# Issuing SyncE's first load before its register moves and before ScalarE's small load

## The chip, the cores and the metric

The kernel runs on one core of one Trainium2 chip. The metric is device time in microseconds (us) of that core. The profiled spans are some 2 us shorter than the timed executions (130.3 against 132.57 us in before). A span here runs from the first instruction of the trace to the last.

## The reference, cut to what matters

The program is an attention block over a set of points (through 32 "inducing" rows) and a feed-forward block with GELU. Only the shapes matter for the change: `x` is 4 x 12480 x 128 in float32, 25.6 MB, it is read once, and an output of the same size is written.

```python
I = np.broadcast_to(inducing[None], (B, m, C))       # m = 32 rows of C = 128
h = mab(I, x)                                        # the inducing rows attend to x
y = mab(x, h)                                        # x attends to the result
# ... then on all 49920 rows: gelu(y @ w_in) @ w_out, w_in 128 x 2048
```

## The kernel before

The first transfers are the subject. The first "pair" of `x` is 32 blocks of 128 rows. SyncE loads half of it in float32 as `x_first`, VectorE casts this half to float16, and GpSimd's queue loads the other half, casting on the way. GpSimd then loads a second pair, and ScalarE loads the small `inducing`.

```python
src = units[0][0].rows_of(x_rows)
nc.sync.dma_start(out=x_first[:, :16, :], in_=src[:, :16, :])      # L295, 1 MB
nc.gpsimd.dma_start(out=x_pair[:, 16:, :], in_=src[:, 16:, :])     # L296, cast on the way
a_load(units[0][2])                                                # L287, GpSimd
# ... identity ...
nc.scalar.dma_start(out=ind_s, in_=inducing)                       # L305, 16 KB
nc.tensor.transpose(indT_ps, ind_s, identity[:M, :M])              # L307
# ... constants on VectorE, 8 warm-up matmuls on TensorE (fill, L359),
#     two casts of x_first (a_cast, L363), then transposes of x (L377) ...
```

The instructions are generated first and reordered afterwards, by a function of the kernel's own source: `loads_ahead` takes the first load or loads of an engine out of the body and puts them into the program's entry block, ahead of the barrier with which the program opens. For each engine it says how many loads, and in front of the first instruction of which kind:

```python
for engine, n, kind in (
    (ET.SP, 1, mybir.InstDrain),
    (ET.Activation, 1, mybir.InstDrain),
    (ET.Pool, 2, mybir.InstEventSemaphore),
):
    moves = [i for i in rest if i.engine == engine][:n]
    ...
    at = min(k for k, i in enumerate(head)
             if i.engine == engine and isinstance(i, kind))   # layout shortened
    head[at:at] = moves
```

In the raw records of before SyncE runs four register moves (at 0.000, 0.070, 0.136 and 0.186 us), then the load (0.256), then the drain that belongs to the barrier (0.691). The results were correct with the load on either side of the moves.

Of the kernel before, what the change touches and what calls it, by code (L numbers as in the profile page):

```python
# [248 lines left out]
def kernel(  # L249
# [742 lines left out]
    with tc.If(flag > 0, preferred_fallthrough_block=False):  # L992
        general(tc, x, moe_w_in, moe_w_out, out, ind_s, identity)
    nc.at_finalize(loads_ahead)
    nc.at_finalize(last_waits_last)
    ET = mybir.EngineType
# [10 lines left out]
def loads_ahead(nc):  # L1007



    entry, body = nc.main_func.blocks[:2]
    head, rest = list(entry.instructions), list(body.instructions)
    ET = mybir.EngineType
    for engine, n, kind in (
        (ET.SP, 1, mybir.InstDrain),
        (ET.Activation, 1, mybir.InstDrain),
        (ET.Pool, 2, mybir.InstEventSemaphore),
    ):
        moves = [i for i in rest if i.engine == engine][:n]
        for i in moves:  # L1020
            assert isinstance(i, mybir.InstDMACopy)
            rest.remove(i)
        at = min(
            k
            for k, i in enumerate(head)
            if i.engine == engine and isinstance(i, kind)
        )
        head[at:at] = moves
    entry.instructions, body.instructions = head, rest
# [296 lines left out]
```

## Time and profile before

| | before |
|---|---|
| time, median of 5 runs | 132.57 us (132.43 to 132.61) |
| profiled span | 130.3 us |
| SyncE's load: issued / first packet / mean landing | 0.256 / 1.257 / 5.24 us |
| GpSimd's first load: first packet / mean landing | 4.795 / 7.79 us |
| last store landed | 130.07 us |

The profile lines that the prediction rests on are shown with it, below. "Issue" of a load is the length of its instruction on the engine that issues it (0.377 us for SyncE's load in before); its data move as packets, which the page counts on 16 transfer engines (128 packets of 8192 bytes for this load). In the raw records such a load has 16 completion records of 4 bytes and 9 ns, and 16 landings, and "mean landing" above is the mean of these 16 times. The GB/s column counts bytes written: GpSimd's load, which casts to float16, shows about half the rate of SyncE's plain one at the same use of the engines (4096 bytes in 0.324 us against 8192 in 0.309). And in a table of stretches a packet counts, with its whole length and all its bytes, in the stretch in which it starts; in a short stretch where packets are slow, the share and the rate are then too high.

### The profile page before, as it was taken

What the parts mean: (1) busy time and instruction counts of PE and PEld (TensorE: products, weight loads), DVE (VectorE), ACT (ScalarE), POOL (GpSimd) and SP (SyncE); (2) the same over time, 40 slices, a digit from 0 to 9 for tenths busy, and PEclk for the clock granted to TensorE, in tenths of its full rate; (3) what the DMA queues carried; (4) which work ended last, traced back from release to release, by engine and by line L of the source; (5) the groups of instructions that cost most, each with busy time, mean ns of one, the idle gap of its engine ahead of it and who ended that gap; (6) DMA issues with size and microseconds to landing.
All of it is one profiled execution on the core that took longest, in us unless ns stands there. A gap on an engine that the chain in (4) does not pass through costs nothing. (4 is left out here: it accounts for less than half of the span.)

```text
span 130.3 us, 3507 instructions
## 1 busy us (share of the span) xinstructions
PE 99.2 (76%) x1365; PEld 57.5 (44%) x1365; DVE 91.6 (70%) x265; ACT 77.1 (59%) x177; POOL 65.2 (50%) x85
## 2 busy tenths in 40 slices
PE   0954878549999999999789899999996698860000
PEld 0342656349465547656544664655453413310000
DVE  1836257432699997999999977999999757993000
ACT  3007064416756888578968889798996285960000
POOL 7910113019453836895753679765198842770000
PEclk9999599965799999999999999999999657998555
DMA  4999999999999999999999999999999999999993
GB/s 131 311 228 214 211 206 211 229 209 214 224 199 219 221 211 322 322 380 377 302 324 330 310 220 288 340 367 418 443 424 419 407 453 418 405 428 430 428 418 125
DMA packets 5666, 40.17 MB, mean 308 GB/s; under 512 B 624, under 2 KB 1936, under 8 KB 2192
## 3 DMA queue, kind: packets, MB, share of 16 engines
q0 software_dynamic: 2848, 13.30, 50.1%
q1 hardware_dynamic: 2752, 26.61, 48.9%
q8 instruction: 11, 0.18, 0.5%
q10 hardware_dynamic: 48, 0.02, 0.1%
q14 instruction: 7, 0.06, 0.1%
HBM read 27.67 MB, written 25.56 MB: 409 GB/s over the span
## 5 line engine op out<-in xcount | busy, mean ns | idle before, releaser
L702 POOL TENSOR_TENSOR pair<-pair,rr 128x512 f32<-128x512 f32 x26 | 26.8, 1042 | 20.6 <-ACT pair L365 17.7
L686 PE MATMUL at<-q,e 128*128 128x512 f16 (+1 forms) x104 | 33.4, 389 | 3.8 <-DVE xT L363 1.2
L377 PE MATMUL tr<-identity_h,xh 128*128 128x128 f16 x392 | 30.3, 232 | 3.3 <-DMA xh<-in_x_dram 3.3
L377 PEld LDWEIGHTS <-xh 128*128 128x128 f16 x392 | 25.2, 105 | 9.9 <-DMA xh<-in_x_dram 4.8
L363 DVE COPY xT<-tr 128x1024 f16<-128x1024 f16 (+1 forms) x36 | 22.6, 645 | 8.9 <-PE tr L377 8.3
L365 ACT ACTIVATE xT<-tr 128x1024 f16<-128x1024 f16 (+1 forms) x16 | 15.7, 980 | 16.5 <-PE tr L377 16.5
L717 DVE TENSOR_TENSOR pair<-at,rr 128x512 f32<-128x512 f32 x36 | 23.3, 676 | 1.1 <-PE at L686 0.4
L287 POOL DMA_DIRECT2D xh<-in_x_dram x15 | 8.3, 555 | 21.4 <-DMA xh<-in_x_dram 14.2
L403 ACT ACTIVATE e<-s 128x512 f16<-128x512 f32 (+1 forms) x28 | 15.3, 546 | 5.6 <-PE s L391 5.1
L638 ACT ACTIVATE e<-s 128x512 f16<-128x512 f32 (+1 forms) x28 | 15.0, 563 | 3.6 <-PE s L626 1.8
L365 ACT ACTIVATE pair<-at 128x512 f32<-128x512 f32 x26 | 15.6, 600 | 1.6 <-PE at L686 1.0
L686 PEld LDWEIGHTS <-e 128*128 128x128 f16 (+1 forms) x104 | 8.7, 103 | 10.3 <-issue 6.9
L417 DVE STREAM_TRANSPOSE e1t<-e 128x256 int32<-128x256 int32 (+1 forms) x28 | 11.1, 399 | 3.0 <-ACT e L403 2.9
L572 POOL TENSOR_TENSOR pt<-pt 128x512 f32<-128x512 f32 (+4 forms) x20 | 12.0, 602 | 2.1 <-DVE rr L661 0.7
L425 PE MATMUL hun<-xh,e1t 128*32 128x128 f16 x392 | 10.7, 225 | 3.1 <-DVE e1t L417 3.0
L717 DVE TENSOR_TENSOR o<-at,rr 128x512 f32<-128x512 f32 (+1 forms) x19 | 10.5, 580 | 3.0 <-PE at L686 2.6
L391 PE MATMUL s<-xT,indT 128*32 128x512 f16 (+1 forms) x108 | 10.5, 376 | 1.6 <-ACT xT L365 0.8
L626 PE MATMUL s<-xT,hT 128*32 128x512 f16 (+1 forms) x100 | 10.2, 417 | 0.5 <-DVE rr L661 0.5
L425 PEld LDWEIGHTS <-e1t 128*32 128x32 f16 x392 | 6.3, 97 | 8.9 <-DVE e1t L417 6.5
L702 POOL TENSOR_TENSOR o<-o,rr 128x512 f32<-128x512 f32 x7 | 7.3, 1042 | 5.4 <-ACT o L365 3.0
L650 PEld LDWEIGHTS <-e 128*128 128x128 f16 (+1 forms) x104 | 5.6, 99 | 4.4 <-issue 1.7
L650 PE MATMUL r<-strand,e 128*128 128x4 f16 (+1 forms) x104 | 6.8, 168 | 0.0
(76 smaller groups left out, 100.6 us busy)
## 6 DMA issues: line engine op xcount, KB each, us to landing
out_dram<-pair SPq DMA_DIRECT2D x8, 2048.0 KB, 15.1
xh<-in_x_dram POOLq DMA_DIRECT2D x11, 1024.0 KB, 28.1
out_dram<-o SPq DMA_DIRECT2D x6, 1024.0 KB, 10.7
out_dram<-spent SPq DMA_DIRECT2D x1, 2048.0 KB, 18.3
x_first<-in_x_dram SPq DMA_DIRECT2D x1, 1024.0 KB, 5.2
xh<-in_x_dram POOLq DMA_DIRECT2D x1, 512.0 KB, 7.1
w_in_h<-in_moe_w_in_dram POOLq DMA_DIRECT2D x1, 512.0 KB, 17.4
w_out_h<-in_moe_w_out_dram POOLq DMA_DIRECT2D x1, 512.0 KB, 19.4
```

Of the source, the lines that this page charges most:

```text
L363: nc.vector.tensor_copy(out=out, in_=in_)
L365: nc.scalar.activation(out=out, in_=in_, func=AF.Copy)
L377: nc.tensor.transpose(tr[:, c - c0, : u.p], xh[: u.p, c, :], identity_h[: u.p, : u.p])
L403: nc.scalar.activation(out=e1[: u.p, : u.nc // 2, :, :], in_=s1[: u.p, : u.nc, :].rearrange("r (a b) i -> r a i b", b=2), func=AF.Exp, sca ...
L417: nc.vector.transpose(out=pairs(e1t)[: u.p, :n], in_=pairs(e1)[: u.p, :n])
L425: nc.tensor.matmul(bt.hun[32 * j : 32 * j + 32, :], e1t[: u.p, c // 2, :, c % 2], xh[: u.p, c, :], start=u.idx == 0 and c < 4, stop=c + 4 ...
L572: nc.gpsimd.tensor_tensor(out=bt.pt[:, :, :, :half], in0=bt.pt[:, :, :, :half], in1=bt.pt[:, :, :, half : 2 * half], op=ALU.add,)
L638: nc.scalar.activation(out=e2[: u.rows, : u.cols], in_=s2[: u.rows, : u.cols], func=AF.Exp, scale=SCALE,)
L650: nc.tensor.matmul(r2[: u.p, ci, : u.nj], e2[: u.rows, ci * u.p : (ci + 1) * u.p], strand[: u.rows, : u.nj], start=True, stop=True,)
L686: nc.tensor.matmul(at[: u.p, : u.nj, :], e2[: u.rows, ci * u.p : (ci + 1) * u.p], bt.q[: u.rows, : u.nj, :], start=True, stop=True,)
L702: nc.gpsimd.tensor_tensor(out=part, in0=part, in1=rr2[: u.p, ci, : u.nj].unsqueeze(2).broadcast_to([u.p, u.nj, 128]), op=ALU.mult,)
L717: nc.vector.tensor_tensor(out=ov[: u.p, ci, :, :], in0=at[: u.p, : u.nj, :], in1=rr2[: u.p, ci, : u.nj].unsqueeze(2).broadcast_to([u.p, u. ...
```

## The change

Its intent is that the program's longest stream, its transfers, starts with its own first load as early as possible: SyncE's load no longer stands behind four register moves, and ScalarE's small load, which used to be issued first, comes second.

```diff
     for engine, n, kind in (
-        (ET.SP, 1, mybir.InstDrain),
+        (ET.SP, 1, mybir.InstRegisterMove),
         (ET.Activation, 1, mybir.InstDrain),
         (ET.Pool, 2, mybir.InstEventSemaphore),
     ):
```

## The prediction

The 0.62 us from the end of an issue to the first packet is the trace's own, the gain comes to 0.256 - 0.06 = 0.20 us, and the weighted time to 132.4 us. Rival (a) supposes that GpSimd's first load can't begin before about 4.8 us, whatever goes before it.

> **What bounds the kernel now.** I read the page first: the engine line, then the DMA rows of the forty slices, then the table of stretches, then the opening and the end in the timeline.
>
> ```profile
> PE 99.2 (76%) x1365; PEld 57.5 (44%) x1365; DVE 91.6 (70%) x265; ACT 77.1 (59%) x177; POOL 65.2 (50%) x85
> ...
> DMA  4999999999999999999999999999999999999993
> ...
> HBM read 27.67 MB, written 25.56 MB: 409 GB/s over the span
> ```
>
> No compute engine is over 76% busy, while the DMA row is full in every slice but the first and the last. The table of stretches gives the share of each (columns: stretch and its length, five engines, granted clock, DMA share, GB/s):
>
> ```profile
> 0.00:1.00 1.00, 0.00 (x0) 0.00 (x0) 0.00 (x0) 0.00 (x0) 0.20 (x4) 1.00 0.00 0
> 1.00:2.00 1.00, 0.00 (x0) 0.00 (x0) 0.18 (x1) 0.00 (x0) 0.93 (x2) 1.00 0.50 92
> 2.00:3.00 1.00, 0.00 (x0) 0.00 (x1) 0.16 (x2) 0.87 (x1) 0.93 (x4) 1.00 0.84 260
> 3.00:5.00 2.00, 1.97 (x6) 0.83 (x7) 1.38 (x14) 0.41 (x1) 2.00 (x4) 1.00 0.97 381
> 5.00:10.00 5.00, 3.56 (x37) 2.15 (x35) 2.88 (x14) 0.21 (x1) 1.91 (x4) 1.00 1.08 223
> ...
> 88.00:126.00 38.00, 24.98 (x237) 10.97 (x234) 26.62 (x82) 21.32 (x55) 18.49 (x20) 0.82 1.01 426
> 126.00:131.00 5.00, 0.00 (x0) 0.00 (x0) 0.00 (x0) 0.00 (x0) 0.00 (x0) 0.50 0.40 162
> ```
>
> The 16 transfer engines idle for the first 1.2 us, ramp to about 2.5 us, and are then full until 126 us (shares over 1.00 are packets that overlap on an engine). The end is theirs too:
>
> ```profile
> 118.70 0.14 DVE failed L979
> ...
> SPq L1321 <- DMA out_dram<-o: 4.2, 2, 2.4
> ```
>
> The first line is the last piece of the chain of compute, over at 118.84 us; the second, from SyncE's own waits, shows it waiting for output stores to land. In the raw records the last store is issued at 118.0 and its last landing is at 130.07, with the span over at 130.28. So the compute chain is some 10 us ahead of the stores, and the program lasts as long as one unbroken stream of transfers: when that stream starts, plus its work. Only the opening can be changed by this edit.
>
> **The opening.** From the timeline (start, length, engine, line, operation):
>
> ```profile
> 0.14 0.42 ACTq L305 DMA_DIRECT2D ind_s<-in_inducing_dram  x1
> ...
> 0.26 0.38 SPq L295 DMA_DIRECT2D x_first<-in_x_dram  x1
> ...
> 1.07 0.72 POOL L296 DMA_DIRECT2D xh<-in_x_dram  x1 [0.61 <-issue]
> ...
> 5.50 1.37 DVE L363 CAST xh<-x_first 128x1024 f16<-128x1024 f32 x2
> ...
> 8.23 1.79 PEld L377 LDWEIGHTS <-xh 128*128 128x128 f16 x32 [2.30 <-DMA xh<-in_x_dram]
> ```
>
> The reader is to see that the changed load is issued at 0.26 and lands just before 5.5, but that the first transposes start only at 8.23, when GpSimd's first load has landed as well. The list of issues says the same:
>
> ```profile
> x_first<-in_x_dram SPq DMA_DIRECT2D x1, 1024.0 KB, 5.2
> xh<-in_x_dram POOLq DMA_DIRECT2D x1, 512.0 KB, 7.1
> ...
> ind_s<-in_inducing_dram ACTq DMA_DIRECT2D x1, 16.0 KB, 2.8
> ```
>
> [...] if one counts from the end of the issue: SyncE's ends at 0.633 and its first packet starts at 1.257, 0.62 us later; ScalarE's ends at 0.562, first packet at 1.187, again 0.62. [...] x_first gives each engine eight 8 KB pieces of 309 ns, they run back to back, and GpSimd's queue starts on an engine only after x_first's completion record there (15 of the 16 engines: 6 ns after). [...] Here SyncE's issue begins inside ScalarE's and takes 0.377 us against some 0.33 us for later lone stores[...].
>
> **The change part by part.** The instruction streams of the five engines are the same in kind and number. On SyncE alone the load steps over four register moves. In the raw records these start at 0.000, 0.070, 0.136 and 0.186 us and take 40, 42, 29 and 29 ns; with the gaps between them the load starts at 0.256.
>
> - Removed ahead of the load: 0.256 us. It should start at about 0.00, its issue end at 0.38, its first packet start at 0.38 + 0.62 = 1.00 instead of 1.257.
> - Added after it: the same four moves, some 0.2 us, before SyncE's drain for the opening barrier. The drain starts at 0.691 now and would start at about the same time. The barrier is collected by GpSimd at 1.496, so nothing there moves.
> - Moved: the small load of ScalarE, issued at 0.137, becomes the second one. It has 32 pieces of 512 bytes, two for each engine, at about 25 ns. Before, they ran in the ramp, where engines were idle anyway. Now they may run behind x_first. Cost in the full stream: 2 x 25 ns + a completion record of 9 ns = 0.06 us on each engine.
>
> If the whole stream slides with its first load, the gain is 0.256 - 0.06 = 0.20 us, or 0.15% of 132.57. It goes through to the end undiminished, because from 2.5 to 126 us there is no idle stretch to swallow it.
>
> Off the path: x_first landing 0.26 us earlier lets VectorE cast earlier, but the transposes wait for GpSimd's load. What shifts those is that load's turn on the engines.
>
> **The rivals.** (a) *GpSimd's first load is not ready.* [...] x_first ending at 4.6 merely leaves the engines idle. Against: its issue ends at 1.79, long before, and 15 engines took it up within 6 ns. For: one engine wrote x_first's completion record at 4.389, and no packet of GpSimd's queue starts anywhere before 4.795, so that engine stood idle for at least 0.4 us with work that should have been there. This would leave 132.5 to 132.6.
>
> (b) *The ramp shortens as well.* The 128 packets of x_first took 45.6 us of engine time against 128 x 0.309 = 39.6 at full rate, and from 1.187 to 2.5 us the engines were only 50% busy: seven began near 1.2, nine not before 2.1, and on those nine a piece of ind_s comes first. If ind_s holds them up, having x_first ahead could win up to half of the 0.65 us lost there: 132.0 to 132.2. Against: pieces of ind_s taking 0.2 to 1.0 us instead of 25 ns look like slow first accesses, which whoever comes first must pay.
>
> (c) *ind_s comes late.* Behind x_first's eight pieces it could land near 5.2 instead of 2.9 us. TensorE transposes it before its eight warm-up matmuls (3.55 us), which end at 6.8 now and have 1.4 us to spare before 8.23; VectorE's set-up and two casts follow the same transposition and end at 6.87. A delay of 2.2 us would push the first transposes back by 0.8 us. But the median x load lands 28 us after its issue, so its queue has many transfers waiting, and the stores are 10 us behind compute: the stream would not run dry. Cost at the end near zero, at worst 0.3 us (132.6 to 132.8).
>
> (d) A share of more than 2% would be 2.65 us, more than the whole of the opening up to full rate. Nothing here has that size.
>
> **Range and chances.** I give half to the clean slide (132.35 to 132.4), 0.3 to rival (a) at about 132.55, 0.1 to (b) at 132.1 and 0.1 to (c) at 132.7: the weighted time is 0.5 x 132.37 + 0.3 x 132.55 + 0.1 x 132.1 + 0.1 x 132.7 = 132.4. Three runs of before spread over 0.18 us, so the range must have that on both sides: 132.1 to 132.7. Within 2% is all but sure: 0.99, with 0.005 for each side.
>
> **What would show it right or wrong.** Right: x_first issued at 0.0, its first packet near 1.0, landed near 5.2; GpSimd's first packets near 4.55; its landing and the first transposes near 8.0; the last store landing 0.2 us earlier; DMA rows otherwise the same. Rival (a): GpSimd's first packets still at 4.8, with an idle gap before. Rival (b): all engines at work before 2 us. Rival (c): ind_s landing after 4.5 us and the first transposes no earlier than 8.3. The prediction is wrong if the end moves by more than 0.4 us either way, or if the load's first packet does not move with its issue.

## The result, and the profile after

The changed kernel took 132.77 us (median of 5, 132.34 to 132.95) against 132.57. The outputs are right. The ratio is 1.0014, with a 95% interval of 0.9994 to 1.0033. A ratio in this document is the mean time of one kernel's fast runs over the mean of the other's in the same rounds, so it is not quite the ratio of the medians quoted. This is "within 2%", as predicted, but 0.07 us outside the predicted range and with no sign of the gain of 0.2 us.

The page of the kernel after, engines, transfer row and bytes:

```profile
PE 98.7 (75%) x1365; PEld 58.6 (45%) x1365; DVE 91.5 (70%) x265; ACT 76.9 (59%) x177; POOL 65.6 (50%) x85
...
DMA  6999999999999999999999999999999999999992
...
HBM read 27.67 MB, written 25.56 MB: 407 GB/s over the span
```

The first digit of the transfer row went from 4 to 6: the engines do start earlier. The last went from 3 to 2, and nothing else moved. The table of stretches of the kernel after (same columns as in the prediction):

```profile
1.00:2.00 1.00, 0.00 (x0) 0.00 (x0) 0.19 (x1) 0.00 (x0) 0.94 (x2) 1.00 0.98 221
2.00:3.00 1.00, 0.00 (x0) 0.00 (x0) 0.16 (x2) 0.88 (x1) 0.92 (x4) 1.00 0.93 331
...
5.00:10.00 5.00, 4.95 (x35) 2.40 (x36) 3.64 (x26) 0.00 (x0) 1.79 (x4) 1.00 1.04 204
...
126.00:131.00 5.00, 0.00 (x0) 0.00 (x0) 0.00 (x0) 0.00 (x0) 0.00 (x0) 0.50 0.43 177
```

By this table the engines were 98% busy instead of 50% from 1 to 2 us, and moved 221 GB/s instead of 92. Shared out over the time in which each packet ran, it is 76% instead of 31%, and 168 GB/s instead of 66. So the first microseconds were won. But from 5 to 10 us, with the same loads and a share that reads full in both, the rate was 204 GB/s instead of 223 (197 instead of 216, shared out). The timeline of the kernel after:

```profile
0.00 0.38 SPq L295 DMA_DIRECT2D x_first<-in_x_dram  x1
0.12 0.39 ACTq L305 DMA_DIRECT2D ind_s<-in_inducing_dram  x1
...
1.06 0.72 POOL L296 DMA_DIRECT2D xh<-in_x_dram  x1 [0.61 <-issue]
...
4.70 0.28 PE L307 MATMUL indT_ps<-identity,ind_s 32*128 32x32 f32 x1 [4.70 <-DMA ind_s<-in_inducing_dram]
...
6.99 0.68 DVE L363 CAST xh<-x_first 128x1024 f16<-128x1024 f32 x1
...
8.52 1.79 PEld L377 LDWEIGHTS <-xh 128*128 128x128 f16 x32 [0.93 <-DMA xh<-in_x_dram]
```

The load is issued at 0.00, but the first transposes of `x` start at 8.52, which is 0.29 us later than in this trace of before (a second one, before2, has 8.99), and they still wait for GpSimd's load. The list of issues (columns: tile, queue, KB, median us from issue to landing) shows which loads became slower:

```profile
x_first<-in_x_dram SPq DMA_DIRECT2D x1, 1024.0 KB, 5.2
xh<-in_x_dram POOLq DMA_DIRECT2D x1, 512.0 KB, 7.4
...
ind_s<-in_inducing_dram ACTq DMA_DIRECT2D x1, 16.0 KB, 4.4
```

GpSimd's first load takes 7.4 us instead of 7.1 and the small one 4.4 instead of 2.8. The end is as it was: the chain of compute of the kernel after is over at 119.6 us,

```profile
119.48 0.14 DVE failed L979
```

and SyncE's waits again end with output stores, some 10 us later:

```profile
SPq L1321 <- DMA out_dram<-o: 4.2, 2, 2.4
```

**From the raw packet records.** The following is my own working on the records of single packets.

*Packets.* In both kernels GpSimd's first load is 128 packets of 4096 written bytes, and a packet usually takes 0.324 us. Before, the median was 0.324 and the longest 0.516. After, the median was 0.326, but eleven took over 0.6 and the longest 1.394. I call time above 0.324 per packet the *excess*: 0.8 engine-us before, 8.8 after. One engine-us is one of the 16 engines for 1 us, so the excess of 8 more is 0.5 us of the whole stream.

*Account of the opening.* From 1 to 9 us I add up what the 16 engines lost, by idling and by packets slower than their usual time:

| kernel | issue of x_first (us) | idle | slow packets | lost in all (engine-us) |
|---|---|---|---|---|
| before | 0.256 | 14.2 | 6.4 | 20.6 |
| after | 0.000 | 4.6 | 18.8 | 23.4 |

Idling fell by 9.6 engine-us (0.60 us for each engine), and slow packets rose by 12.4 (0.77 us). So the earlier start was used up within the first 9 us. A plainer count, of all time above the median of a packet's queue and size, gives nearly the same: 14.4 idle and 7.0 slow before, 4.9 and 19.8 after.

*Work curve.* I give each packet the usual time of its queue and size, add these up over the program, and compare the times at which two kernels have done the same work. After led before by 0.22 us at 5.6 us. At 8.7 us it was 0.09 behind, and from 12 to 45 us it was a constant 0.14 behind.

### The profile page after: what moved, and what is told of

Its sections match the earlier page's. It is cut to its first block, busy times and chain, and to the rows that moved or that the text cites. A ratio compares the mean times of both kernels' runs of the same rounds, so it can differ in the third digit from the quotient of the medians.

```text
span 130.9 us, 3507 instructions
## 1 busy us (share of the span) xinstructions
PE 98.7 (75%) x1365; PEld 58.6 (45%) x1365; DVE 91.5 (70%) x265; ACT 76.9 (59%) x177; POOL 65.6 (50%) x85
## 5 line engine op out<-in xcount | busy, mean ns | idle before, releaser
L702 POOL TENSOR_TENSOR pair<-pair,rr 128x512 f32<-128x512 f32 x26 | 26.8, 1042 | 19.6 <-ACT pair L365 16.7
L686 PE MATMUL at<-q,e 128*128 128x512 f16 (+1 forms) x104 | 32.4, 378 | 3.5 <-DVE xT L363 1.2
L377 PE MATMUL tr<-identity_h,xh 128*128 128x128 f16 x392 | 31.2, 236 | 3.2 <-DMA xh<-in_x_dram 3.1
L377 PEld LDWEIGHTS <-xh 128*128 128x128 f16 x392 | 26.0, 106 | 9.8 <-DMA xh<-in_x_dram 4.8
L365 ACT ACTIVATE xT<-tr 128x1024 f16<-128x1024 f16 (+1 forms) x16 | 15.7, 980 | 18.2 <-PE tr L377 18.1
L425 PE MATMUL hun<-xh,e1t 128*32 128x128 f16 x392 | 11.2, 233 | 3.0 <-DVE e1t L417 3.0
L626 PE MATMUL s<-xT,hT 128*32 128x512 f16 (+1 forms) x100 | 9.3, 380 | 0.5 <-DVE rr L661 0.5
## 6 DMA issues: line engine op xcount, KB each, us to landing
out_dram<-o SPq DMA_DIRECT2D x6, 1024.0 KB, 10.2
w_out_h<-in_moe_w_out_dram POOLq DMA_DIRECT2D x1, 512.0 KB, 19.2
```

Source lines behind the costliest of these rows:

```text
L365: nc.scalar.activation(out=out, in_=in_, func=AF.Copy)
L377: nc.tensor.transpose(tr[:, c - c0, : u.p], xh[: u.p, c, :], identity_h[: u.p, : u.p])
L425: nc.tensor.matmul(bt.hun[32 * j : 32 * j + 32, :], e1t[: u.p, c // 2, :, c % 2], xh[: u.p, c, :], start=u.idx == 0 and c < 4, stop=c + 4 ...
L686: nc.tensor.matmul(at[: u.p, : u.nj, :], e2[: u.rows, ci * u.p : (ci + 1) * u.p], bt.q[: u.rows, : u.nj, :], start=True, stop=True,)
L702: nc.gpsimd.tensor_tensor(out=part, in0=part, in1=rr2[: u.p, ci, : u.nj].unsqueeze(2).broadcast_to([u.p, u.nj, 128]), op=ALU.mult,)
```

## The experiments

**Theories.** T1: the slide was there, and scatter hid it. T2, rival (a) of the prediction: GpSimd's queue isn't ready until about 4.8 us. T3: the small load, now moved in among the pieces of `x_first`, or the later set-up work that follows from it, costs what the slide gains. T4: packets early in a stream are slow, and a stream that starts earlier has more of them; the start moves, but not the moment at which the full rate is reached. All four are suppositions for the runs to test.

The texts before each run use other names. "Readiness" is T2, "set-up" is T3, and "cold access" is a stricter T4: a fixed stock of slow first packets, paid by whoever comes first. From sp_mid on they add a fifth, "early take-up", here T5: GpSimd's packets are slow when its load is taken up too soon after its issue. It is T2 in a weaker form: the queue can be used early, but not at full speed.

The eighteen runs went in five sets, each on one chip together with runs of the kernel before, whose medians were 132.53, 132.57, 132.50, 132.52 and 132.46 us. Idle and slow engine-us are those of the account above, always from 1 to 9 us.

### The same two kernels again: before2, after2, after3

No edit. This tells how much of the first result was scatter (T1).

> The kernel before, unchanged, for the spread of its own trace and time. All theories: ratio 1.000 within 0.002; x_first's first packet near 1.26 us; the 128 packets of GpSimd's first load about 1 us of engine time over their floor of 128 x 0.324 us in all (it was 0.8); that load's 16 landings with a mean near 7.8 us. If the excess is instead 5 to 10 us here too, the loss seen after the change is chance and not the change.

> The changed kernel, unchanged, once more. If the loss is of the change: GpSimd's first load starts near 4.0 us, has again 6 to 11 us of engine time over its floor (8.8 in the first trace), and its landings have a mean of 7.7 to 7.9 us, no earlier than before; ratio 0.999 to 1.003. If the first trace was an accident: excess of 0 to 3 us, landings with a mean near 7.3 us, ratio near 0.997.

> The changed kernel a third time, for its time: the first five runs gave a ratio of 1.0014, the six of the second 1.0002. If those were scatter about nothing: 0.999 to 1.002 here, GpSimd's first load with an excess of 8 to 10 and a mean landing of 7.7 to 7.9 us once more.

Measured: before2 132.54 us, ratio 0.9999 (0.9984 to 1.0015). after2 132.56, ratio 1.0002 (0.9986 to 1.0017). after3 132.51, ratio 0.9987 (0.9962 to 1.0013). Over all sessions the median is 132.58 for 17 runs of the changed kernel; in the five later sets it is 132.52 for 57 runs of before. So the 0.2 us of loss in the first session was mostly scatter. By times alone a gain of 0.1% can't be ruled out: after3 has just that ratio.

The traces decide it, because they repeat. The account is 21.9 engine-us lost for before2 (idle 10.1, slow 11.8), 23.4 for after2 (4.3 and 19.1) and 21.9 for after3 (4.0 and 17.9). The excess of GpSimd's first load was 2.8 in before2, 9.7 in after2 and 7.6 in after3. On the work curve after2 and after3 led by 0.21 and 0.26 us at 5.6 us, and at 8.7 us they were 0.08 behind and level. Measured against before2 instead of before, the three traces of after were 0.02, 0.03 and 0.12 us ahead at 8.7 us, and 0.08 behind, 0.07 behind and 0.03 ahead at 12 us: the lead is gone either way. One stretch of the after2 table shows it, 5 to 8 us:

```profile
5.00:8.00 3.00, 3.00 (x8) 0.95 (x8) 2.54 (x24) 0.00 (x0) 1.26 (x3) 1.00 1.05 197
```

and the same stretch of the first trace of before:

```profile
5.00:8.00 3.00, 1.79 (x5) 0.38 (x3) 1.77 (x12) 0.00 (x0) 1.37 (x3) 1.00 1.13 229
```

It is 197 GB/s against 229 (190 in the first trace of after, 205 in after3, 221 in before2). T1 falls as an explanation: three traces in three sessions lose the lead at the same place.

### The order alone: order_only, order_only2

Before, but ScalarE's small load goes behind ScalarE's drain. SyncE's load stays behind its moves at 0.257 us, and the small load is issued at 0.223; its packets come after those of `x_first` have begun.

```diff
-        (ET.Activation, 1, mybir.InstDrain),
+        (ET.Activation, 1, mybir.InstEventSemaphore),
```

> SyncE's load stays behind its four moves (start 0.26 us); ScalarE's small load goes behind ScalarE's drain, so that x_first is still the first transfer. This is the order without the 0.26 us. Order theory (the ramp shortens because no piece of ind_s comes before x_first): x_first's engines are all at work by about 2.0 us and its landings have a mean near 5.0 us, against 5.24 before and 4.72 after. Shift theory (what came early came from the 0.26 us): a mean of 5.2 us and nine engines idle until 2.1 us as before. For the time: cold-access theory (a fixed stock of slow first packets is paid by whoever comes first) says 0.999 to 1.002; the readiness theory [...] says a first load with half of the excess, 3 to 5 us, and 0.998 to 1.001.

> The order without the 0.26 us, again. In its first run the stream was 0.19 us ahead from 8 to 45 us and lost 0.36 us at 46.5 to 48.5 us in a burst of slow packets. If the lead belongs to the order: first landing of GpSimd's load again at a mean of 7.5 to 7.7 us and a work curve 0.1 to 0.3 us ahead at 30 us. If the burst at 47 us is chance: it is 0 to 2 us of engine time this time, the curve stays ahead to the end, and the profiled time is 132.2 to 132.4. If every lead is taken back before the stores begin: burst again 3 us or more. Ratio 0.998 to 1.002 either way.

Measured: 132.62 us, ratio 1.001 (0.9988 to 1.0032), and 132.70, ratio 1.0019 (0.9998 to 1.004). No gain in the time. But in the opening this half of the change did what the prediction asked of the whole. The account fell to 19.2 and 19.5 engine-us lost (idle 9.5 in both, slow 9.7 and 10.0), the excess of GpSimd's first load stayed at 1.0 and 0.8, and the load landed 0.19 and 0.18 us earlier than before. The work curve leads by 0.19 and 0.18 us, unchanged from 5.6 to 45 us. Then it is 0.16 and 0.17 *behind* from 48.5 us to the end. The second stretch table of order_only2, 45 to 48.5 us:

```profile
45.00:48.50 3.50, 3.50 (x48) 1.47 (x46) 3.18 (x9) 2.99 (x9) 1.04 (x1) 1.00 1.07 201
```

and of before:

```profile
45.00:48.50 3.50, 3.50 (x60) 1.41 (x48) 3.22 (x8) 2.99 (x9) 1.35 (x2) 1.00 1.08 220
```

The same share of the engines carries 201 GB/s instead of 220. The packet records there hold 5.9 and 6.3 engine-us of slow packets in the two traces, against 1.5 in before. This is just before the first packets of the first output store (issued at 45.34 us in before and 44.65 in after, first packet at 48.85 and 48.13). Order alone therefore gains in the opening and pays at a second place. What makes packets slow there is not known.

### Half the moves, and more than the moves: sp_mid, sp_later

sp_mid puts the load behind two of the four moves, with the small load behind ScalarE's drain; it is issued at 0.088 us. sp_later puts it behind SyncE's own drain, at 0.337 us, after the small load's issue at 0.222.

```diff
-        (ET.SP, 1, mybir.InstDrain),
-        (ET.Activation, 1, mybir.InstDrain),
+        (ET.SP, 1, mybir.InstRegisterMove),         # sp_mid: before the third move
+        (ET.Activation, 1, mybir.InstEventSemaphore),
# sp_later: mybir.InstEventSemaphore on both lines
```

> A dose: x_first behind two of SyncE's four moves (start near 0.14 us, between the 0.00 of the change and the 0.26 of before), ScalarE's small load behind ScalarE's drain. If the slow packets of GpSimd's first load come from taking that queue up too early, the loss falls with the start: first packets of that load at 4.2 to 4.4 us, excess over the floor 2 to 7 us of engine time (9 at a start of 4.0 to 4.1, 2.8 at 4.41, 0.9 at 4.53), mean landing 7.6 to 7.8. If they come from chance or from the order alone: excess 0.5 to 1.5 like the two runs of the order alone, mean landing 7.45 to 7.55. Ratio 0.998 to 1.003 on either theory.

> The other end of the dose: x_first behind SyncE's drain as well (start 0.3 to 0.5 us). Early-take-up theory: GpSimd's first load starts at 4.6 to 4.9 us with an excess under 1.5 us, mean landing 7.6 to 7.9. If a burst of slow packets before the first store (46 to 48 us) goes with the order rather than with the early lead, it is there again with 4 us or more. Ratio 0.999 to 1.004.

Measured: sp_mid 132.91 us, ratio 1.002 (0.9994 to 1.0047); sp_later 132.69, ratio 1.000 (0.9973 to 1.0027). sp_mid behaves like after: idle 4.5, slow 21.6, excess of GpSimd's first load 10.2. sp_later behaves like before: 14.0, 7.4 and 1.3. Between issues at 0.0 and 0.34 us the time didn't move measurably, while idle time was exchanged for slow packets. The step between the two behaviours lies between 0.088 us (sp_mid) and 0.257 us (order_only).

### GpSimd alone first: x_late

Before, with SyncE's load left out of the entry block and made to wait for a small write by GpSimd, so that GpSimd's queue starts with nothing in front of it but the small load.

```diff
-    nc.sync.dma_start(out=x_first[:, :16, :], in_=src[:, :16, :])
     nc.gpsimd.dma_start(out=x_pair[:, 16:, :], in_=src[:, 16:, :])
     ...
+    nc.gpsimd.memset(x_first[:, :1, :8], 0.0)
+    nc.sync.dma_start(out=x_first[:, :16, :], in_=src[:, :16, :])
# and in loads_ahead: (ET.SP, 0, mybir.InstDrain)
```

> The kernel before, with x_first issued only after a small GpSimd memset behind the identity, near 3 us, so that its first packet could come near 4 us and the transfer engines stand empty until GpSimd's first load is ready. It measures when that load can start. Readiness theory: no packet of GpSimd's queue before 4.4 us, though its issue ended at 1.8. Cold-access theory: its packets start between 2 and 3 us, the early ones slow (5 to 15 us of engine time over the floor in all), so the lead of x_first was never limited by GpSimd. Pass-through: the stream starts its bulk 1 to 3 us later than before (first packets of ind_s aside), and the last landings should be later by as much as the work curve is late at 10 us, to within 0.3 us: ratio 1.005 to 1.02.

Measured: 136.66 us (135.51 to 138.27), ratio 1.035 (1.0302 to 1.0398). The run of 138.27 is slow and is in this ratio; the other three are 2.8% above the median of before, so it is slower without that run too. GpSimd's queue moved its first packet at 2.49 us, 0.71 us after its issue ended at 1.784. That refutes T2 as the prediction put it: this queue moved packets long before 4.8 us. It doesn't refute T5, since these packets came soonest of all after their issue and were slow. Its first load's packets were slow here too, by 11.5 engine-us, with no `x_first` in front of them, so it isn't the sharing with SyncE's load that slows them. The loss of time has another cause that the experiment brought with it. The timeline of x_late:

```profile
2.97 3.89 SPq L301 DMA_DIRECT2D x_first<-in_x_dram  x1
```

SyncE's issue, 0.38 us elsewhere, took 3.89 us here, and the first packet of `x_first` came at 10.0 us, 3.2 us after the issue's end (0.62 in before). The compute chain then ended at 126.7 us rather than 118.8, so the end of x_late is not to be compared with the others. Why the issue took that long was not followed.

### GpSimd's issues earlier and later: pool_early, pool_late

After, with GpSimd's two loads ahead of its own memsets, or with neither in the entry block.

```diff
-        (ET.Pool, 2, mybir.InstEventSemaphore),
+        (ET.Pool, 2, mybir.InstMemset),             # pool_early
+        (ET.Pool, 0, mybir.InstEventSemaphore),     # pool_late
```

> The changed kernel, and GpSimd's first two loads ahead of its four constants, so that the first is issued near 0.2 instead of 1.06 us. Readiness theory: [...] excess falls from about 9 to under 2 us of engine time, the mean landing of the first load from 7.8 to 7.2 to 7.3 us, and the stream ends 0.4 to 0.5 us earlier (ratio 0.996 to 0.998). Cold-access theory: the excess stays 6 to 11 us, the mean landing stays within 0.15 us of 7.8, ratio 0.999 to 1.002. Set-up theory (ind_s comes late, so VectorE's set-up and casts run beside this load and slow it): also no change, since ind_s is as late as before.

> The changed kernel with GpSimd's first two loads behind the opening barrier: issue near 1.7 to 1.8 instead of 1.06 us. Readiness theory: all of the delay shows: first packets near 4.7 us or later instead of 4.05, or packets that start at 4.05 and stall, the landings of that load with a mean 0.5 to 0.7 us later (8.3 to 8.5), ratio about 1.003 to 1.005. Cold-access theory: the load is still issued 2 us before x_first ends, so it starts at 4.0 to 4.1 again, mean landing 7.7 to 7.9, ratio 0.999 to 1.002.

Measured: pool_late 132.54 us, ratio 0.9996 (0.9975 to 1.0017). The issue came only 0.38 us later (1.435), and the excess of GpSimd's first load was 8.7, as in after. Its mean landing was 7.99, between what readiness (8.3 to 8.5) and cold access (7.7 to 7.9) asked for. It tells little.

pool_early 136.24 us, ratio 1.0281 (1.026 to 1.0302), slower, and for a reason that I hadn't thought of. Its timeline:

```profile
13.37 0.20 POOL masks.py:197 MEMSET identity<- 128x128 f32 x1 [11.17 <-POOLq L1310]
```

In the raw records GpSimd's drain of the opening barrier, 0.183 us long in before, began here at 1.257 and lasted 11.87 us. It ended at 13.12, and the second of the two loads now ahead of it landed last at 13.01. All engines waited for that barrier: from 0 to 13 us TensorE, VectorE and ScalarE ran nothing in this run. SyncE's drain, behind the issue of `x_first`, was not long in this way (0.123 us in before, 0.007 in after and in pool_early). The run is still of use twice. First, its table of stretches:

```profile
5.00:8.00 3.00, 0.00 (x0) 0.00 (x0) 0.00 (x0) 0.00 (x0) 0.00 (x0) 1.00 1.07 201
```

No engine computes, GpSimd issues nothing between 2 and 13 us, and the transfers run at 201 GB/s, as slow as in after. The account is 3.1 idle and 16.9 slow. So packets are slow in this run without compute and without GpSimd's later issues. But they were not as slow as in after: the excess of GpSimd's first load, issued 0.32 us earlier here, was 4.8 instead of 8.8, and its mean landing was 7.49 instead of 7.81. This fits neither readiness (under 2) nor cold access (6 to 11). And the lead did not vanish here: the work curve was 0.21 us ahead of before at 8.7 us and 0.25 at 12 us, before the barrier cost it. Second, the curve is 3.96 us late from 18 us on and 4.04 us late at the end. So this large shift did go through to the end, nearly one to one.

### The small load and the set-up work: ind_late, setup_early

ind_late is after with the small load out of the entry block altogether; it lands at 11.55 to 12.31 us. setup_early is after with the transposition of `ind_s` and its copy moved behind the warm-up and the casts, so that the later landing holds nothing up.

```diff
-        (ET.Activation, 1, mybir.InstDrain),
+        (ET.Activation, 0, mybir.InstDrain),        # ind_late
# setup_early: indT_ps, its transpose and its copy to indT go into a function
# that is called after the second cast of x_first
```

> The changed kernel, with ScalarE's small load not in the opening at all but behind the barrier, so that no piece of it lies in front of or among x_first's first pieces. If ind_s among x_first is what slows GpSimd's first load: excess of that load falls from 9 to under 3 us of engine time, mean landing 7.4. If it has nothing to do with it (early take-up): excess 7 to 11, mean landing 7.7 to 7.9, ratio 0.999 to 1.003.

> The changed kernel, with the transposition of ind_s and its copy behind TensorE's warm-up and VectorE's two casts, so that nothing in the set-up waits for the late ind_s (warm-up from 2 us, casts from 5.2 us). Set-up theory (VectorE's set-up and casts, pushed to 5.0 to 8.3 us by the late ind_s, slow GpSimd's first load): its excess over the floor falls from about 9 to under 3 us of engine time and the mean landing from 7.81 to 7.4, ratio 0.996 to 0.998. Readiness and cold-access theories: excess stays 6 to 11 us, mean landing 7.7 to 7.9, ratio 0.999 to 1.002.

Measured: ind_late 133.89 us, ratio 1.0099 (1.0047 to 1.0152): some 1% longer. setup_early 132.57, ratio 1.0013 (0.9989 to 1.0037). The stretch of ind_late:

```profile
5.00:8.00 3.00, 0.00 (x0) 0.00 (x0) 0.00 (x0) 1.13 (x1) 1.25 (x3) 1.00 1.08 199
```

and of setup_early:

```profile
5.00:8.00 3.00, 0.98 (x3) 0.18 (x1) 1.43 (x5) 0.00 (x0) 1.67 (x3) 1.00 1.06 197
```

Both have slow packets just as after (excess 10.6 and 9.3), though in ind_late the small load is gone from among the pieces and in setup_early the set-up work is. T3 falls. As in x_late, a load that left the entry block was issued slowly: ScalarE's issue took 4.72 us in ind_late, 0.39 in after (SyncE's in x_late 3.89, 0.38 in after). ind_late also bounds the slack of compute: a start delayed to 12 us does reach the end, by about 1.3 us.

### A small packet first: primer

After, with GpSimd's first load cut into one block and fifteen, to see whether a few small packets take the slowness on themselves.

```diff
-    nc.gpsimd.dma_start(out=x_pair[:, 16:, :], in_=src[:, 16:, :])
+    nc.gpsimd.dma_start(out=x_pair[:, 16:17, :], in_=src[:, 16:17, :])
+    nc.gpsimd.dma_start(out=x_pair[:, 17:, :], in_=src[:, 17:, :])
# and in loads_ahead: Pool 3
```

> The changed kernel, with GpSimd's first load cut in two: a first sixteenth (128 rows of 512 bytes, on all 16 engines) and then the rest, so that the queue's first packets are small ones and the rest is issued some 0.5 us later. If the cost is that of the queue's first packets on each engine, whatever they carry: the small ones stall, the rest runs at its floor, and the rest's excess is under 3 us of engine time with a mean landing of 7.6 to 7.9. If packets are slow because the load is taken up too soon after its issue: the rest, issued later, is as slow or slower (excess 8 to 14 us, landing after 7.9). Ratio 0.999 to 1.004.

Measured: 132.68 us, ratio 1.001 (0.9983 to 1.0036). The small packets ran from 3.97 us; 115 of the 128 took 40 to 42 ns, the others 46 to 480. The large ones that followed were slow all the same: an excess of 7.0, two of them 1.8 and 1.9 us long. So the slowness is not used up by the first packets of the queue.

### More of the first pair through SyncE: x20, before_x20, x24, and again x20_2, x24_2

SyncE takes 20 (or 24) of the 32 blocks and GpSimd 12 (or 8); the second cast is longer. x20 and x24 are made from after, before_x20 from before. GpSimd's queue then begins later, after 5 us.

```diff
-    nc.sync.dma_start(out=x_first[:, :16, :], in_=src[:, :16, :])
-    nc.gpsimd.dma_start(out=x_pair[:, 16:, :], in_=src[:, 16:, :])
+    nc.sync.dma_start(out=x_first[:, :20, :], in_=src[:, :20, :])      # x24: 24
+    nc.gpsimd.dma_start(out=x_pair[:, 20:, :], in_=src[:, 20:, :])
     ...
+        c1 = 8 if c0 == 0 else 20       # a_cast: 0 to 8 and 8 to 20
```

> The changed kernel, with x_first taking 20 of the first pair's 32 column blocks instead of 16 and GpSimd's first load the other 12. x_first ends some 0.6 us later, so GpSimd's queue is taken up near 4.7 us, 3.6 us after its issue, as in before, though the stream still starts at 1.0. If the slow packets come from taking GpSimd's load up too soon after its issue: excess of that load under 2 us of engine time (9 at a start of 4.0 to 4.1), and the work curve keeps its lead: 0.25 to 0.45 us ahead of before from 10 to 45 us. If every early start of the stream is paid back at the next transfer whatever its time: excess 7 to 11, curve level or behind. Ratio 0.997 to 0.999 if the lead lasts to the end; 0.999 to 1.002 if it is lost at GpSimd's load or before the first store.

> The control: the same 20 and 12 in the kernel before. GpSimd's load is taken up near 5.2 us; both theories: excess under 2, the work curve within 0.12 us of before, ratio 0.999 to 1.001.

> The changed kernel with 24 and 8: GpSimd's load taken up near 5.3 us. If the time since its issue matters, as in x20: excess under 1.5, the curve 0.25 to 0.45 us ahead from 10 to 45 us. The last cast is twice as long and starts later, but compute is ahead of the stores by 10 us, so it costs nothing. Ratio 0.997 to 1.001.

> x20 again, for its time and its opening. If it truly beats both kernels: ratio again 0.996 to 0.999, 132.1 to 132.4 us; slow packets of 4 to 8 us gone again (under 3 us of engine time in all, against 9 to 10 in the changed kernel), slow and idle engine time of 1 to 9 us together 19 to 22. If its first result was the scatter of the kernel before on that chip (132.24 to 133.07 there): 0.999 to 1.001.

> x24 again. If it truly beats both kernels: 0.995 to 0.998, 131.9 to 132.4 us. Its opening wasted as much as that of the changed kernel (23.1 us of engine time) and x_first itself had slow packets at 4 to 6 us: if that repeats (2 us or more of slow packets on SyncE's queue at 4 to 6 us), slow packets at that time don't belong to GpSimd's queue.

| run | median (us) | ratio (95%) | first GpSimd packet | its excess | idle | slow | lost |
|---|---|---|---|---|---|---|---|
| before_x20 | 132.39 | 0.9981 (0.9956 to 1.0006) | 5.28 | 1.1 | 10.0 | 12.4 | 22.4 |
| x20 | 132.28 | 0.9973 (0.9948 to 0.9999) | 5.20 | 0.9 | 2.3 | 18.2 | 20.5 |
| x20_2 | 132.09 | 0.9965 (0.9926 to 1.0004) | 5.08 | 1.4 | 4.0 | 15.6 | 19.6 |
| x24 | 132.15 | 0.9965 (0.9938 to 0.9992) | 5.61 | 0.4 | 6.5 | 16.6 | 23.1 |
| x24_2 | 132.24 | 0.9973 (0.9935 to 1.0011) | 5.28 | 0.5 | 7.5 | 16.0 | 23.4 |

GpSimd's packets are no longer slow once they begin after 5 us, as T5 had said (under 2, and under 1.5 for x24). But the slow packets did not go away. In x20 they sit in 1 to 3 us (14.7 engine-us, against 9.1 in after), and the earlier start keeps a part of its gain: the mean landing of the second GpSimd load is 12.66 and 12.61 us in x20 and x20_2 against 12.78 in before_x20, where after had 12.88 against 12.75 in before; in x24 and x24_2 SyncE's own pieces are slow between 4 and 6 us (4.9 engine-us in each).

This doesn't show that the slowness at 4 to 7 us moves to whichever queue is active. The pieces of x24 are 12 KB long, not 8, and they never settle: shared out over the time in which they ran, they lose 1.6 and 1.5 engine-us from 3 to 4 us too, where those of after lose 0.4. There is no run with 24 blocks and a late start to compare with; with 20 blocks, SyncE's pieces lose as much from 4 to 6 us in before_x20, which starts late (1.8), as in x20 and x20_2 (1.7 in each).

On the work curve x20 and x20_2 were 0.09 and 0.14 us ahead of before at 44 us, and 0.19 and 0.17 ahead at 120 us; before_x20 was 0.03 behind and 0.02 ahead. That is less than the 0.25 to 0.45 us that had been expected, but here a part of the earlier start does reach the end.

All four runs of the changed kernel with the larger `x_first` are ahead of before, by about 0.3%, on two chips, though two of the four intervals reach just over 1; before_x20 is 0.2% ahead and unclear. These are the best versions found, and by little. The account fits at most x20, which loses 20.5 and 19.6 engine-us; x24 loses as much as after and is as fast as x20. Where x24's time comes from is open.

## Why the prediction was right or wrong

**Right: everything up to the first packets.** The load started at 0.000 and its issue ended at 0.381. Its first packet came at 1.024 (predicted 1.00), 0.64 us after the issue's end. The issue took 0.381 us although it began 0.12 us before ScalarE's; in before, where it began inside ScalarE's, it took 0.377. So the 0.05 us that it has over the later stores (0.332) do not come from its being second. `x_first` landed 0.5 us earlier in the mean (4.72 against 5.24). The barrier didn't move: GpSimd's first semaphore instruction of it was at 1.484, before at 1.496. The class, within 2%, was right for the reason given in (d).

**Right in place, and free, as rival (c) had it.** `ind_s` landed from 3.73 to 4.56 us (1.58 to 2.90 before), and the warm-up and VectorE's set-up came later for it: in the stretch from 5 to 8 us of after2 shown above TensorE is busy throughout. That cost nothing at the end: setup_early, which takes this delay out, measured 1.0013. The first transposes did come later, at 8.52, but they waited for GpSimd's load and not for the set-up.

**Right as a fact, of no use: rival (b).** The ramp shortened, by more than the load's 0.256 us. From 1 to 2 us the engines were 76% busy instead of 31% (shared out exactly), 16 packets were first under way at once at 1.62 us instead of 2.36, and GpSimd's first packet came at 3.995, not at the 4.55 of the prediction. I had given this 0.1, and expected that it would carry through. The objection noted against it showed too: in after, with `x_first` in front, the first 13 of its packets took 0.55 to 1.15 us (median of all 128: 0.309), and no piece of `ind_s` more than 0.035, where in before the longest had taken 1.03.

**Wrong: the step from the start to the end.** The step that failed is "It goes through to the end undiminished, because from 2.5 to 126 us there is no idle stretch to swallow it." The premise, no idle stretch, is true. The conclusion doesn't follow, because this stream lost time without idling: by packets that took longer. The three traces of after idle for 4.0 to 4.6 engine-us and lose 17.9 to 19.1 to slow packets; the two of before idle for 14.2 and 10.1 and lose 6.4 and 11.8. What was gained by not idling was paid back in slow packets. The lead of 0.21 to 0.26 us at 5.6 us was gone at 8.7. GpSimd's landing on the slowest engine, predicted near 8.0, came at 8.48, 8.54 and 8.27 in the three traces (8.19 and 8.95 in the two of before), and its mean landing was 7.81, 7.81 and 7.72 in the three traces against 7.79 and 7.88 in the two of before. pool_early's shift of 3.96 us, on the other hand, arrived as 4.04.

**Rival (a) named the right place for the wrong reason.** It said that GpSimd's first load would not profit. It didn't, but not because its engines stood idle until 4.8 us. In after one engine took up GpSimd's queue at 3.995, 6 ns after the first completion record of `x_first` at 3.989. x_late has packets there at 2.49. A weaker form of the rival, T5, is still standing (see below).

**Two readings of the prediction were off.** It took shares over 1.00 for packets that overlap on an engine. That is a part of it: shared out exactly, the 1.08 of before from 5 to 10 us is 1.04, and the rest comes from counting a packet where it starts. And the small load did not run behind `x_first` but among its pieces: in after all 32 pieces of `ind_s` started between 2.70 and 3.87 us, before the first completion record of `x_first` at 3.99.

**Wrong: the last store.** "The last store landing 0.2 us earlier" was in fact at 130.69, 130.19 and 130.53 in the three traces of after, against 130.07 and 130.34 in two of before. That one figure scatters by 0.5 us within one kernel, so it can't judge a step of 0.2.

**The range was too narrow for one session.** I allowed 0.18 us on each side from three runs of before. The five runs of after spread over 0.61 us in the first session.

**What stays open.** What makes the packets slow is not settled. Refuted as stated: readiness of GpSimd's queue only at 4.8 us (x_late), set-up work and compute as the whole cause (setup_early, pool_early), the small load among the pieces (ind_late), GpSimd's later issues as the whole cause (pool_early), a few first packets of the queue (primer), a fixed stock of slow packets (6.4 engine-us in before, 21.6 in sp_mid), and chance (three traces).

Two descriptions are left. T4: when the first packet of `x_first` starts at 1.00 to 1.11 us (after, sp_mid) rather than at 1.26 to 1.39 (before, order_only, sp_later), idle time comes back as slow packets. It describes this and doesn't explain it, and x20 goes against it: its start is as early, and it keeps a part of the gain. T5, early take-up, orders the excess of GpSimd's first load by the time from the end of its issue to its first packet, in the raw records:

| first packet after the issue's end (us) | runs | excess (engine-us) |
|---|---|---|
| 0.71 | x_late | 11.5 |
| 1.84 | pool_late | 8.7 |
| 2.21 to 2.35 | after, after2, after3, ind_late, setup_early, sp_mid | 7.6 to 10.6 |
| 2.49 | pool_early | 4.8 |
| 2.62 | before2 | 2.8 |
| 2.74 to 3.84 | order_only, order_only2, sp_later, before, before_x20, x20, x20_2, x24, x24_2 | 0.4 to 1.4 |

(primer is left out because its load is cut.) So the excess falls from about 9 to about 1 between 2.4 and 2.7 us after the issue. This is a connection in these runs, not a cause that was tested: the clock time of the first packet orders them almost as well, and only pool_early, whose packets start as early as those of after and are half as slow, speaks for the time since the issue. A run that issues GpSimd's load earlier without the wait of its drain would decide; there is none. T5 doesn't account for the slow packets of `x_first` itself from 1 to 3 us. Also open is the second place, just before the first store, that took back the 0.19 us of order_only.

## What to carry to other kernels

An earlier start of a stream of transfers need not be kept, even if the engines idle less: here a lead of 0.21 to 0.26 us at 5.6 us was lost to slow packets within 9 us. Check this with GB/s over short stretches after the start, not with the first packet's time and not with the busy share, which read full here with slow packets too (1.04 at 204 GB/s in after, 1.08 at 223 in before, from 5 to 10 us). When a gain is smaller than the scatter of the runs, follow it through the trace as a lead at equal work, and see where the lead is lost. Look at what an opening barrier waits for before loads go ahead of it: with two of GpSimd's loads ahead of its drain, the drain took 11.87 us in pool_early, against 0.183 in before.
